# Attention, then a feed-forward network: the row of maxima transposed by VectorE, the ninth key tile added by GpSimd

## The chip, the cores and the metric

The kernel runs on one core of a Trainium2 chip. The core has five engines that each work through a queue of their own in order: TensorE (PE; its weight loads are shown apart as PEld), VectorE (DVE), ScalarE (ACT), GpSimd (POOL) and SyncE (SP), which here only issues transfers. They meet through semaphores. The metric is device microseconds of one execution.

## What is computed

Two stages, all in float32. The first is attention with pooled queries, for 8 batches of 8 heads, with 1152 keys of 64 numbers; two neighbouring queries are averaged, so 576 queries are left:

```python
q_pool = q.reshape(B, H, S // factor, factor, D).mean(axis=3)
scores = scale * np.matmul(q_pool, k.transpose(0, 1, 3, 2))
scores = scores - np.max(scores, axis=-1, keepdims=True)
attn = np.exp(scores)
attn = attn / (np.sum(attn, axis=-1, keepdims=True) + 1e-09)
return np.matmul(attn, v).astype(np.float32)
```

The second stage takes the result as 4608 tokens of 512 numbers through `h = x @ w_in`, `g = h - tanh(h)` and `g @ w_out`, with 2048 hidden numbers. The inputs are scaled so that the scores are large, which is why the maximum of each row has to be taken away before the exponential.

## The kernel before

**Pairs and units.** Heads are worked in pairs: 32 pairs, the two heads of a pair on partitions 0 to 63 and 64 to 127. A pair is worked in two halves of 288 queries. A half is nine key tiles of 128 keys; each gets one step of scores (`scores`), two units of a clock that the code counts. So a half is 18 units and a pair 36. All work beside the scores is hung on units by `add(u, f)`, some of it ahead of the unit's scores (`first`, then `early`), the rest behind. The table `units`, `row`, `steps` and `spots` of the last loop gives the unit of each piece of work, counted from the first unit of the pair that it is for: with -62 the work is done 62 units earlier, beside another pair's scores. `InOrder` makes every engine keep the order in which the code was run.

**Scores.** The numbers are split in a high and a low part (`hi` on ScalarE, `lo` on VectorE, which is `kq` less `hi`), and a step of scores is four kinds of product, for two heads each: `hi` by `hi`, `hi` by `lo`, `lo` by `hi`, and last `ones_k` by `mb`, which adds the negative maximum of each query to its column. `mb` holds the row of maxima as two rows per head, its high and its low part. ScalarE then takes the exponential out of PSUM into `p_f`.

**Maxima.** They come from products of the high parts alone (`max_part`): five query tiles by three key chunks, 15 a pair, hung on units of the pair before. VectorE reduces each over its keys (`mx<-ps`). `max_rows` then makes the row: VectorE reduces to ten columns (`nm`), TensorE transposes them with the identity into a PSUM tile (`ps<-ident,nm`), ScalarE and VectorE split the transpose in two parts (`mt`), and SyncE writes them to `m_dram` and reads them back to `mb` in four transfers.

**PSUM.** Scores, maxima, the transposed row, the outputs and the weight conversion all take their tiles from one pool of four (`ps_a`, two banks each). Whoever wants a fifth waits for the one to come free that was chosen when the program was built.

**Output and sums.** At a half's last unit TensorE multiplies the nine `p_f` by `v` (`pv`). GpSimd adds `p_f` tiles three by three, and the last group is two (`z_part`). After the second half's `pv`, `z_sums` sums over the keys by products with ones: four rounds, over the three sums `z` and over the ninth `p_f` itself, for two halves and two heads each. GpSimd also adds the two queries of a pool (`query_sums`, `kq<-q_n`), except for the first pair, and does part of the weight conversion (`w`, `w_hl`) that is spread over the pairs for the second stage.

**SyncE.** All loads and stores go through its queue in the order of the code.

Of the kernel before, what the change touches and what calls it, by code (L numbers as in the profile page):

```python
# [8 lines left out]
F32 = mybir.dt.float32  # L9
F32R = mybir.dt.float32r  # L10
I32 = mybir.dt.int32
AF = mybir.ActivationFunctionType
ALU = mybir.AluOpType
AX = mybir.AxisListType
# [29 lines left out]
def kernel(  # L44
# [17 lines left out]
    nc = tc.nc  # L62
    P = 128
    B, NP, _, _, SQ = q.shape
# [10 lines left out]
    dram = ctx.enter_context(tc.tile_pool(name="scratch", bufs=1, space=DRAM))  # L75

    ident = const.tile([P, P], F32, name="ident")
# [5 lines left out]
    ones = const.tile([P, 32], F32, name="ones")  # L83
# [3 lines left out]
    x_dram = dram.tile([NP, P, NTOK], F32, name="x_dram")  # L87
    z_dram = dram.tile([B, NP, 2, SQ], F32, name="z_dram")
    r_dram = dram.tile([B, NP, 2, SQ], F32, name="r_dram")
    m_dram = dram.tile([2, 10, 2, P], F32, name="m_dram")  # L90
    wi_dram = dram.tile([NF, P, 2, NP, P], F32, name="wi_dram")
    wo_dram = dram.tile([NF, P, 2, DM], F32, name="wo_dram")

# [41 lines left out]
    t, n = chunks.pop()  # L135
# [4 lines left out]
    with ExitStack() as actx:  # L140

        sm = actx.enter_context(tc.tile_pool(name="sm", bufs=2))
        op = actx.enter_context(tc.tile_pool(name="op", bufs=1))
# [7 lines left out]
        pe, act, dve, pool, sp = (InOrder(tc, e) for e in (nc.tensor, nc.scalar, nc.vector, nc.gpsimd, nc.sync))  # L151

        HQ = SQ // 2
        CH = S // 3
# [5 lines left out]


        mb = [op.tile([P, SQ], F32R, name=f"mb{i}") for i in range(2)]
        ones_k = op.tile([P, P], F32R, name="ones_k")
        for x in (*mb, ones_k):
            nc.gpsimd.memset(x.bitcast(F32), 0.0)
        for h in range(2):
            nc.gpsimd.memset(ones_k[64 * h:64 * h + 2].bitcast(F32), 1.0)


        at, first, early = {}, {}, {}  # L170

        def banks(dtype=F32):
            return ps_a.tile([P, 2, 512], dtype, name="ps")
# [3 lines left out]
        def add(u, f, *args, at=at):  # L177
            at.setdefault(u, []).append(lambda: f(*args))
# [22 lines left out]
        def query_sums(pi, eng):  # L201

            w = pairs[pi]
            eng.tensor_tensor(w.kq[:, 0:SQ], w.q_n[:, 0], w.q_n[:, 1], op=ALU.add)
            w.mx = sm.tile([P, 5, 2, 3], F32, name="mx")
            w.hi = hl.tile([P, KQ], F32R, name="hi")
            w.lo = hl.tile([P, KQ], F32R, name="lo")

# [8 lines left out]
        def max_part(u, pi, t, c):  # L217


            w = pairs[pi]  # L220
            ps = banks()
            q0 = min(t * P, SQ - P)
            mv = slice(SQ + c * CH, SQ + (c + 1) * CH)
            for h in range(2):
                r = slice(64 * h, 64 * h + 64)
                pe.matmul(ps[:, h, 0:CH], w.hi[r, q0:q0 + P], w.hi[r, mv], start=True, stop=True)
            add(u + 1, lambda: dve.tensor_reduce(w.mx[:, t, :, c], ps[:, :, 0:CH], axis=AX.X, op=ALU.max), at=first)

        def max_rows(u, pi, steps):

            w = pairs[pi]
            nm = sm.tile([P, 10], F32, name="nm")
            dve.tensor_reduce(nm, w.mx.rearrange("p t h c -> p (t h) c"), axis=AX.X, op=ALU.max, negate=True)
            mt = sm.tile([10, 2, P], F32R, name="mt")
            md = m_dram[w.i]

            def turn():
                w.ps_t = banks()[0:10, 0, 0:P]
                pe.transpose(w.ps_t, nm, ident)

            def hi():
                act.activation(mt[:, 0], w.ps_t, AF.Copy)

            def lo():
                dve.tensor_tensor(mt[:, 1], w.ps_t, mt[:, 0].bitcast(F32), op=ALU.subtract)

            def there():
                sp.dma_start(md, mt.bitcast(F32))

            def back():  # L250
                by_head = md.rearrange("(t h) s n -> h s t n", h=2)
                for h in range(2):
                    rows = w.mb[64 * h:64 * h + 2].bitcast(F32)
                    sp.dma_start(rows[:, 0:4 * P].rearrange("s (t n) -> s t n", n=P), by_head[h, :, 0:4])
                    sp.dma_start(rows[:, 4 * P:], by_head[h, :, 4, 5 * P - SQ:])
            add(u + 1, turn, at=first)
            add(u + 2, hi, at=first)
            add(u + 3, lo, at=first)
            add(u + steps[0], there)
            add(u + steps[1], back)  # L260

        def scores(w, half, kt, p):

# [21 lines left out]
        def pv(u, hf):  # L285

            w, ps = hf.w, banks()
            hf.o = ps[:, 0]
            for kt in range(KT):
                for h in range(2):  # L290
                    pe.matmul(hf.o[64 * h:64 * h + 64, 0:HQ], w.v[:, h, kt], hf.p[kt][:, h], start=(kt == 0),
                              stop=(kt == KT - 1), tile_position=(0, 64 * h))
            add(u + 1, o_out, w, hf, at=first)
            w.halves.append(hf)
            if hf.n == 1:
                z_sums(u, w, ps[:, 1])

        def z_sums(u, w, ps):

            parts = [[*hf.zs[:2], hf.p[-1], hf.zs[2]] for hf in w.halves]  # L300
            for g in range(4):
                for n in range(2):
                    for h in range(2):
                        r = 64 * h + 32 * n
                        pe.matmul(ps[r:r + 32, 0:HQ], ones, parts[n][g][:, h], start=(g == 0), stop=(g == 3), tile_position=(0, r))
            add(u + 1, z_out, u + 1, w, ps, at=first)

        def o_out(w, hf):
# [93 lines left out]
        for i, blk in enumerate(blocks):  # L402
            u = U * (i - 2) + 5 if i else 23
# [17 lines left out]
        for i, t in enumerate((wi, wi, wi, wo, wi, wo)):  # L421
            f = len(t)
# [3 lines left out]

        for pi in range(n_pair):
            u = pi * U
            units = dict(load=-80, query_sums=-62, hi=-55, lo=-36, load_v=-30)
            row, steps = -19, (5, 11)  # L430

            spots = [x for half, us in ((-54, (2, 4, 8, 10, 12, 14, 16)), (-36, (2, 4, 8, 10, 14, 16)))
                     for x in [(early, half)] + [(at, half + i) for i in us]]
            if pi == 0:
                units.update(load=-70, query_sums=-62, hi=-60, lo=-41, load_v=-40)
                spots = [(at, -60 + i) for i in range(15)]
                row, steps = -43, (3, 4)
            if pi == 1:
                units.update(load=-104)
            add(u + units["load"], load, pi)  # L440
            add(u + units["query_sums"], query_sums, pi, dve if pi < 1 else pool)
            for c in range(0, KQ, SQ):
                add(u + units["hi"], hi_part, pi, c, c + SQ)
            add(u + units["lo"], lo_part, pi)
            for i, (when, x) in enumerate(spots):
                add(u + x, max_part, u + x, pi, i // 3, i % 3, at=when)
            add(u + units["load_v"], load_v, pi)
            add(u + row, max_rows, u + row, pi, steps)

        def run(u, at=at):  # L450

            while at.get(u):
                at[u].pop(0)()

        for u in range(min(at), 0):
            run(u, first)
            run(u, early)
            run(u)
        z_groups = {kts[-1]: kts for kts in ((0, 1, 2), (3, 4, 5), (6, 7))}
        for u in range(end + 60):  # L460
            run(u, first)
            run(u, early)
            n, r = divmod(u, G)
            if u < end and r % 2 == 0:
                if r == 0:
                    hf = Half()
# [18 lines left out]
    pe, pool, sp = (InOrder(tc, e) for e in (nc.tensor, nc.gpsimd, nc.sync))  # L485
# [81 lines left out]
    for ci, (t0, n) in enumerate(chunks):  # L567
        x_h, x_l, _ = xs
        po = []
        for fc in range(NF):  # L570
# [3 lines left out]
            load = []  # L574
            if ci + 1 < len(chunks):
# [3 lines left out]
                load = [xs[2][(fc - x) // 3][i] for i, x in ((3, 3), (0, 0), (1, 2), (2, 2)) if (fc - x) % 3 == 0 and 0 <= fc - x < 3 * NP]  # L579
            for f in load:  # L580
                f()
            g = hidden(x_h, x_l, n, fc)
# [44 lines left out]
```

## Time and profile before

| | us |
|---|---|
| runs | 1634.25 to 1634.59, median 1634.48 |
| the profiled execution | 1634.2 |
| its span, first to last instruction | 1632.4 |
| TensorE busy | 1611.2 (99%) |
| VectorE, ScalarE, GpSimd busy | 1226.8, 1023.4, 873.3 |

TensorE's granted clock is full (1.000) over the span. The attention stage reaches to about 835 us, the feed-forward network takes the rest. In the timeline a row gives start and length in us, the engine, the line, the operation, the tiles written and read, and how many neighbouring instructions of one kind are merged in it; idle time before it stands in brackets, with what ended it. `L37` is the line of `InOrder`, so groups are told apart by their tiles. On TensorE the records of neighbouring matmuls overlap, so the time that one costs is read from start to start.

### The profile page before, as it was taken

What the parts mean: (1) busy time and instruction counts of PE and PEld (TensorE: products, weight loads), DVE (VectorE), ACT (ScalarE), POOL (GpSimd) and SP (SyncE); (2) the same over time, 40 slices, a digit from 0 to 9 for tenths busy, and PEclk for the clock granted to TensorE, in tenths of its full rate; (3) what the DMA queues carried; (4) which work ended last, traced back from release to release, by engine and by line L of the source; (5) the groups of instructions that cost most, each with busy time, mean ns of one, the idle gap of its engine ahead of it and who ended that gap; (6) DMA issues with size and microseconds to landing.
All of it is one profiled execution on the core that took longest, in us unless ns stands there. A gap on an engine that the chain in (4) does not pass through costs nothing.

```text
span 1632.4 us, 32106 instructions
## 1 busy us (share of the span) xinstructions
PE 1611.2 (99%) x12576; PEld 1246.3 (76%) x12576; DVE 1226.8 (75%) x1725; ACT 1023.4 (63%) x1865; POOL 873.3 (53%) x694
## 2 busy tenths in 40 slices
PE   6999999999999999999999999999999999999999
PEld 3777777777777777777778888888888888888898
DVE  7877778787777777777648776777777777777786
ACT  2656665666556656665566666666665766666786
POOL 2776767667667676676754243434343342423332
PEclk9999999999999999999999999999999999999999
DMA  3343443443434434344546111101010111000000
GB/s 142 121 139 117 140 134 108 127 130 133 127 108 142 134 114 126 123 140 146 157 177 229 39 39 35 31 26 53 26 53 26 39 40 39 27 33 20 33 21 27
DMA packets 72664, 147.86 MB, mean 91 GB/s; under 512 B 11136, under 2 KB 36672, under 8 KB 72512
## 3 DMA queue, kind: packets, MB, share of 16 engines
q1 hardware_dynamic: 72512, 145.80, 27.3%
q8 instruction: 99, 1.62, 0.4%
q14 instruction: 53, 0.43, 0.1%
HBM read 109.49 MB, written 36.27 MB: 89 GB/s over the span
## 4 chain that ended last, share of the span: by engine, by line
PE 97%; DVE 2%; ACT 0%; DMA 0%; issue 0%; ACTq 0%
PE ps L37 49%; PE ps_h L37 24%; PE ps_o L37 24%; DVE mx L37 1%; DMA q_n<-in_q_dram 0%; ACT hi L37 0%; ACT p_f L37 0%; DVE lo L37 0%; DVE kq L37 0%; DVE w L37 0%; DVE ps L37 0%; ACT x L562 0%; ACT z_s L37 0%; ACT mt L37 0%; DVE nm L37 0%
## 5 line engine op out<-in xcount | busy, mean ns | idle before, releaser
L37 DVE TENSOR_REDUCE mx<-ps 128x2 f32<-128x768 f32 x480 | 434.8, 951 | 139.0 <-PE ps L37 138.9
L37 POOL TENSOR_TENSOR g_lo<-g_s,g_hi 128x512 fp32r<-128x512 f32 (+1 forms) x160 | 190.7, 1192 | 483.1 <-ACT g_hi L530 445.0
L37 ACT ACTIVATE p_f<-ps 128x576 f32<-128x576 f32 x576 | 362.7, 650 | 83.5 <-PE ps L37 67.4
L37 POOL TENSOR_TENSOR z<-p_f 128x576 f32<-128x576 f32 x192 | 275.2, 1433 | 236.7 <-ACT p_f L37 236.7
L37 PE MATMUL ps<-hi 64*128 64x288 f32 (+1 forms) x2112 | 318.0, 355 | 13.4 <-ACT hi L37 8.3
L37 PE MATMUL ps_h<-x,wi 128*128 128x512 f32 (+1 forms) x1440 | 318.3, 370 | 0.0
L37 PE MATMUL ps_o<-wo,g_hi 128*128 128x512 f32 x1008 | 311.7, 391 | 0.0
L37 PE MATMUL ps<-p_f,v 128*64 128x288 f32 x2304 | 293.5, 409 | 0.1
L37 PEld LDWEIGHTS ps_h<-x,wi 128*128 128x128 f32 x1440 | 253.3, 188 | 50.3
L37 PEld LDWEIGHTS ps<-hi 64*128 64x128 f32 x2112 | 195.8, 188 | 79.8 <-DVE mx L37 22.9
L37 PEld LDWEIGHTS ps<-p_f,v 128*64 128x64 f32 x2304 | 159.8, 137 | 113.7 <-ACT p_f L37 12.2
L519 ACT ACTIVATE g_u<-ps_h 128x512 f32<-128x512 f32 (+1 forms) x160 | 88.8, 555 | 236.3 <-PE ps_h L37 236.3
L524 DVE SCALAR_TENSOR_TENSOR ps_w<-g_u,ps_h 128x512 f32<-128x512 f32 (+1 forms) x160 | 103.2, 645 | 157.6 <-ACT g_t L520 157.0
L37 PEld LDWEIGHTS ps_o<-wo,g_hi 128*128 128x128 f32 x1008 | 187.7, 188 | 39.0
L37 PE MATMUL ps_o<-wo,g_lo 128*128 128x512 f32 x504 | 196.4, 390 | 0.0
L37 POOL TENSOR_TENSOR z<-z,p_f 128x576 f32<-128x576 f32 x128 | 183.1, 1431 | 10.0
L37 ACT ACTIVATE o_s<-ps 128x288 f32<-128x288 f32 x64 | 26.3, 411 | 231.8 <-PE ps L37 231.8
L37 PE MATMUL ps<-lo,hi 64*128 64x288 f32 x1152 | 171.2, 294 | 0.0
L37 PE MATMUL ps<-hi,lo 64*128 64x288 f32 x1152 | 171.1, 293 | 0.0
L37 PE MATMUL ps<-mb,ones_k 64*128 64x288 f32 x1152 | 170.6, 292 | 0.0
L529 DVE COPY_PREDICATED g_s<-g_m,g_t 128x512 f32<-128x512 int32 (+1 forms) x160 | 115.1, 719 | 16.7 <-DVE g_s L528 0.5
L527 DVE SCALAR_TENSOR_TENSOR ps_w<-g_s,ps_w 128x512 f32<-128x512 f32 (+1 forms) x160 | 102.9, 643 | 16.6 <-ACT g_m L523 0.5
(70 smaller groups left out, 2248.3 us busy)
## 6 DMA issues: line engine op xcount, KB each, us to landing
q_n<-in_q_dram SPq DMA_DIRECT2D x32, 576.0 KB
kq<-in_k_dram SPq DMA_DIRECT2D x32, 576.0 KB
v<-in_v_dram SPq DMA_DIRECT2D x32, 576.0 KB
x_dram<-o_s SPq DMA_DIRECT2D x32, 288.0 KB
out_dram<-o_s SPq DMA_DIRECT2D x34, 256.0 KB
w_raw<-in_moe_w_in_dram SPq DMA_DIRECT2D x16, 512.0 KB
wi_dram<-w_hl SPq DMA_DIRECT2D x16, 512.0 KB
w_raw<-in_moe_w_out_dram SPq DMA_DIRECT2D x16, 512.0 KB
```

Of the source, the lines that this page charges most:

```text
L37: ins = self.tc.keep_in_program_order(f(*args, **kwargs))
L519: nc.scalar.activation(u, h, AF.Square)
L524: nc.vector.scalar_tensor_tensor(w, u, -P0, h, op0=ALU.add, op1=ALU.mult)
L527: nc.vector.scalar_tensor_tensor(w, s2, P2, w, op0=ALU.add, op1=ALU.mult)
L529: last = nc.vector.copy_predicated(s1, m.bitcast(I32), th).ins
```

## The change

`max_rows` no longer uses TensorE, ScalarE or `m_dram`. VectorE writes the ten columns into a zeroed tile of 32 columns, `nm`, and transposes it in blocks of 32 by 32 into `tr`. Column c of `nm` then lies in rows c, 32 + c, 64 + c and 96 + c of `tr`, and SyncE copies it from there to `mb`: ten transfers, one for each head and query tile, of four (or two) pieces of 32 numbers. The row is no longer split: `nm` is written in the rounded type that TensorE reads, `mb` holds one row per head, and `ones_k` has one row of ones per head. The transfers are hung 3 units after the reduction (1 for the first pair).

`z_part`'s last group becomes three tiles, and `z_sums` has three rounds. The loads of `q` and `k` move from unit -80 to -86, and the query sums from -62 to -71 (the second pair keeps -104 and -62, the first its own).

```diff
-        def max_rows(u, pi, steps):
+        def max_rows(u, pi, step):
             w = pairs[pi]
-            nm = sm.tile([P, 10], F32, name="nm")
-            dve.tensor_reduce(nm, w.mx.rearrange("p t h c -> p (t h) c"), axis=AX.X, op=ALU.max, negate=True)
-            mt = sm.tile([10, 2, P], F32R, name="mt")
...
-                pe.transpose(w.ps_t, nm, ident)
...
+            nm, tr = nms[w.i], sm.tile([P, 32], F32, name="tr")
+            dve.tensor_reduce(nm[:, 0:10], w.mx.rearrange("p h t c -> p (h t) c"), axis=AX.X, op=ALU.max, negate=True)
+            dve.transpose(tr, nm.bitcast(F32))
 
             def back():
+                for t in range(5):
+                    for h in range(2):
+                        row, c = w.mb[64 * h:64 * h + 1].bitcast(F32), 5 * h + t
+                        if t < 4:
+                            sp.dma_start(row[:, t * P:(t + 1) * P].rearrange("p (g n) -> p g n", n=32), tr[c:P:32])
+                        else:
+                            sp.dma_start(row[:, t * P:].rearrange("p (g n) -> p g n", n=32), tr[P - (SQ - t * P) + c:P:32])
+            add(u + step, back)
...
-            parts = [[*hf.zs[:2], hf.p[-1], hf.zs[2]] for hf in w.halves]
-            for g in range(4):
+            for g in range(3):
...
-            units = dict(load=-80, query_sums=-62, hi=-55, lo=-36, load_v=-30)
-            row, steps = -19, (5, 11)
+            units = dict(load=-86, query_sums=-71, hi=-55, lo=-36, load_v=-30)
+            row, step = -19, 3
...
-        z_groups = {kts[-1]: kts for kts in ((0, 1, 2), (3, 4, 5), (6, 7))}
+        z_groups = {kts[-1]: kts for kts in ((0, 1, 2), (3, 4, 5), (6, 7, 8))}
```

How this moves instructions is seen at three places. The first is TensorE between the two halves of a pair, the end of the first half's `pv` (64 rows, 288 queries) and the second half's first maxima (384 keys) and scores. Before:

```order
L37 MATMUL ps_4228<-p_f_4190,v_3761 64x288 x2
L37 MATMUL ps_4228<-p_f_4207,v_3761 64x288 [waits Activation_49]
L37 MATMUL ps_4228<-p_f_4207,v_3761 64x288
L37 MATMUL ps_4251<-ident_60,nm_4222 10x128 [waits DVE_49,PE_49]
L37 MATMUL ps_4255<-hi_4173 128x384 [waits PE_49,Activation_49]
L37 MATMUL ps_4255<-hi_4173 128x384
```

And now, for another pair:

```order
L37 MATMUL ps_1195<-p_f_1154,v_719 64x288 x2
L37 MATMUL ps_1195<-p_f_1169,v_719 64x288 [waits Activation_49]
L37 MATMUL ps_1195<-p_f_1169,v_719 64x288
L37 MATMUL ps_1220<-hi_1055 128x384 [waits PE_49,Activation_49]
L37 MATMUL ps_1220<-hi_1055 128x384
```

The transpose with the identity is gone, and with it the PSUM tile `ps_4251`.

The second place is a little later in the same half: its second step of scores, its second tile of maxima and the beginning of its third step. Before:

```order
L37 MATMUL ps_4274<-hi_3414 128x288 [waits Activation_49]
L37 MATMUL ps_4274<-hi_3414 128x288
L37 MATMUL ps_4274<-lo_3415,hi_3414 128x288 x2
L37 MATMUL ps_4274<-hi_3414,lo_3415 128x288 x2
L37 MATMUL ps_4274<-mb0_116,ones_k_118 128x288 x2
L37 MATMUL ps_4284<-hi_4173 128x384 [waits DVE_49]
L37 MATMUL ps_4284<-hi_4173 128x384
L37 MATMUL ps_4289<-hi_3414 128x288 [waits Activation_49]
```

And now:

```order
L37 MATMUL ps_4265<-hi_3327 128x288 [waits DVE_49]
L37 MATMUL ps_4265<-hi_3327 128x288
L37 MATMUL ps_4265<-lo_3328,hi_3327 128x288 x2
L37 MATMUL ps_4265<-hi_3327,lo_3328 128x288 x2
L37 MATMUL ps_4265<-mb0_115,ones_k_119 128x288 x2
L37 MATMUL ps_4275<-hi_4086 128x384 [waits Activation_49]
L37 MATMUL ps_4275<-hi_4086 128x384
L37 MATMUL ps_4290<-hi_3327 128x288 [waits DVE_49]
```

The order of the matmuls is the same, but the tiles come from others: the second tile of maxima waited for VectorE and the third step for ScalarE; now it is the other way round.

The third place is GpSimd's queue in a second half and up to the next half's first adds. Before:

```order
L37 TENSOR_TENSOR z_1648<-p_f_1602,p_f_1617 128x576
L37 TENSOR_TENSOR z_1648<-z_1648,p_f_1632 128x576
L37 TENSOR_TENSOR z_1700<-p_f_1651,p_f_1662 128x576
L37 TENSOR_TENSOR z_1700<-z_1700,p_f_1677 128x576
L37 TENSOR_TENSOR z_1733<-p_f_1703,p_f_1718 128x576
L37 TENSOR_TENSOR w_hl_1750<-w_1_1410,w_hl_1750 128x512
L37 TENSOR_TENSOR z_1847<-p_f_1799,p_f_1813 128x576
```

And now, again for another pair:

```order
L37 TENSOR_TENSOR z_1281<-z_1281,p_f_1262 128x576
L37 TENSOR_TENSOR z_1326<-p_f_1284,p_f_1295 128x576
L37 TENSOR_TENSOR z_1326<-z_1326,p_f_1311 128x576
L37 TENSOR_TENSOR z_1376<-p_f_1329,p_f_1344 128x576
L37 TENSOR_TENSOR z_1376<-z_1376,p_f_1359 128x576
L37 TENSOR_TENSOR kq_1277<-q_n_1276 128x576
L37 TENSOR_TENSOR w_hl_1374<-w_1_1029,w_hl_1374 128x512
L37 TENSOR_TENSOR z_1474<-p_f_1422,p_f_1440 128x576
```

The last `z` has a second add, and the query sum `kq`, which stood between the first and the second group of a first half, now stands between the halves.

More of the change, by code (lines that the diff above doesn't have):

```diff
@@ L89 @@
     r_dram = dram.tile([B, NP, 2, SQ], F32, name="r_dram")
-    m_dram = dram.tile([2, 10, 2, P], F32, name="m_dram")
     wi_dram = dram.tile([NF, P, 2, NP, P], F32, name="wi_dram")
@@ L162 @@
         mb = [op.tile([P, SQ], F32R, name=f"mb{i}") for i in range(2)]
+        nms = [op.tile([P, 32], F32R, name=f"nm{i}") for i in range(2)]
         ones_k = op.tile([P, P], F32R, name="ones_k")
-        for x in (*mb, ones_k):
+        for x in (*nms, *mb, ones_k):
             nc.gpsimd.memset(x.bitcast(F32), 0.0)
         for h in range(2):
-            nc.gpsimd.memset(ones_k[64 * h:64 * h + 2].bitcast(F32), 1.0)
+            nc.gpsimd.memset(ones_k[64 * h:64 * h + 1].bitcast(F32), 1.0)
         at, first, early = {}, {}, {}
@@ L204, in query_sums @@
             eng.tensor_tensor(w.kq[:, 0:SQ], w.q_n[:, 0], w.q_n[:, 1], op=ALU.add)
-            w.mx = sm.tile([P, 5, 2, 3], F32, name="mx")
+            w.mx = sm.tile([P, 2, 5, 3], F32, name="mx")
             w.hi = hl.tile([P, KQ], F32R, name="hi")
@@ L226, in max_part @@
                 pe.matmul(ps[:, h, 0:CH], w.hi[r, q0:q0 + P], w.hi[r, mv], start=True, stop=True)
-            add(u + 1, lambda: dve.tensor_reduce(w.mx[:, t, :, c], ps[:, :, 0:CH], axis=AX.X, op=ALU.max), at=first)
-        def max_rows(u, pi, steps):
+            add(u + 1, lambda: dve.tensor_reduce(w.mx[:, :, t, c], ps[:, :, 0:CH], axis=AX.X, op=ALU.max), at=first)
+        def max_rows(u, pi, step):
             w = pairs[pi]
-            nm = sm.tile([P, 10], F32, name="nm")
-            dve.tensor_reduce(nm, w.mx.rearrange("p t h c -> p (t h) c"), axis=AX.X, op=ALU.max, negate=True)
-            mt = sm.tile([10, 2, P], F32R, name="mt")
-            md = m_dram[w.i]
-            def turn():
-                w.ps_t = banks()[0:10, 0, 0:P]
-                pe.transpose(w.ps_t, nm, ident)
[L241 to L248, printed above, removed]
-            def back():
[L251 to L260, printed above, removed]
@@ L304, in z_sums @@
                         r = 64 * h + 32 * n
-                        pe.matmul(ps[r:r + 32, 0:HQ], ones, parts[n][g][:, h], start=(g == 0), stop=(g == 3), tile_position=(0, r))
+                        pe.matmul(ps[r:r + 32, 0:HQ], ones, w.halves[n].zs[g][:, h], start=(g == 0), stop=(g == 2),
+                                  tile_position=(0, r))
             add(u + 1, z_out, u + 1, w, ps, at=first)
@@ L436 @@
                 spots = [(at, -60 + i) for i in range(15)]
-                row, steps = -43, (3, 4)
+                row, step = -43, 1
             if pi == 1:
-                units.update(load=-104)
+                units.update(load=-104, query_sums=-62)
             add(u + units["load"], load, pi)
@@ L447 @@
             add(u + units["load_v"], load_v, pi)
-            add(u + row, max_rows, u + row, pi, steps)
+            add(u + row, max_rows, u + row, pi, step)
         def run(u, at=at):
```

## The prediction

> **What bounds the kernel now.** I read the page first: the busy shares, then the chain of work that ended last.
>
> ```profile
> PE 1611.2 (99%) x12576; PEld 1246.3 (76%) x12576; DVE 1226.8 (75%) x1725; ACT 1023.4 (63%) x1865; POOL 873.3 (53%) x694
> ...
> PE 97%; DVE 2%; ACT 0%; DMA 0%; issue 0%; ACTq 0%
> ```
>
> TensorE is busy 99% of the span and is 97% of the chain, so a microsecond taken off TensorE's queue is a microsecond off the time, as long as nobody else becomes late. "Busy" hides short waits, though, because a late matmul's record is only a longer one. So I measure slots, from the start of one instruction to the start of the next. The view of busy time by stretches shows one regular pair (columns: stretch, length, then busy time and count of PE, PEld, DVE, ACT, POOL; granted clock; DMA share; GB/s).
>
> ```profile
> 387.34:412.53 25.19, 25.19 (x283) 18.18 (x280) 19.24 (x23) 15.35 (x27) 17.86 (x13) 1.00 0.39 126
> ```
>
> A pair takes 25.19 us, and GpSimd works 17.9 us of it. The diff leaves the second half of the program (the FFN) as it is, so the question is what a pair will take. TensorE's timeline of that pair (start, length, what):
>
> ```profile
> 386.26 0.67 PE L37 MATMUL ps<-p_f,ones 128*32 128x288 f32 x8
> 386.74 0.67 PE L37 MATMUL ps<-z,ones 128*32 128x288 f32 x8
> 387.34 0.58 PE L37 MATMUL ps<-hi 64*128 64x384 f32 x4
> ...
> 389.48 0.56 PE L37 MATMUL ps<-hi 64*128 64x384 f32 x4
> 389.87 0.30 PE L37 MATMUL ps<-lo,hi 64*128 64x288 f32 x2
> 390.00 0.29 PE L37 MATMUL ps<-hi,lo 64*128 64x288 f32 x2
> ...
> 393.94 4.59 PE L37 MATMUL ps<-p_f,v 128*64 128x288 f32 x36
> 398.46 0.28 PE L37 MATMUL ps<-ident,nm 128*10 128x128 f32 x1
> 398.67 0.57 PE L37 MATMUL ps<-hi 64*128 64x384 f32 x4
> ...
> 399.88 0.29 PE L37 MATMUL ps<-mb,ones_k 64*128 64x288 f32 x2
> 400.17 0.70 PE L37 MATMUL ps<-hi 64*128 64x384 f32 x4
> 400.71 0.29 PE L37 MATMUL ps<-lo,hi 64*128 64x288 f32 x2
> ...
> 405.94 4.59 PE L37 MATMUL ps<-p_f,v 128*64 128x288 f32 x36
> 410.45 1.18 PE L37 MATMUL ps<-z,ones 128*32 128x288 f32 x16
> 411.45 0.67 PE L37 MATMUL ps<-p_f,ones 128*32 128x288 f32 x8
> ```
>
> **The change part by part.** The sum is made against the profiled execution's own 1634.2 us (span 1632.4 and 1.8 around it); the median of the runs, 1634.48, is 0.3 above it.
>
> *Fourth round of row sums.* The round over the ninth tile, `p_f,ones`, goes from 386.26 to 386.74: 0.48 us. Every one of the 32 pairs has one: 32 x 0.48 = 15.4 us less.
>
> *Transpose on TensorE.* It occupies 398.46 to 398.67, 0.21 us. Of 32, the first lies in the start-up, where TensorE waits anyway: 31 x 0.21 = 6.5 us less.
>
> *The tile it held.* The first half's scores and maxima go from 387.34 to 393.94: 6.60 us, with seven tiles of maxima. The second half, with eight, goes from 398.67 to 405.94: 7.27 us. A tile of maxima costs 389.87 - 389.48 = 0.39, less the 0.13 that two score matmuls take (389.87 to 390.00): 0.26. So 6.86 would do, and 0.41 is waiting. Two waits are visible: the maxima at 400.17 could have started at 400.01 (399.88 + 0.13), 0.16; and the next step takes 0.54 (400.17 to 400.71) instead of 0.39 or 0.40, about 0.14. Their cause stands on VectorE and ScalarE:
>
> ```profile
> 399.15 0.96 DVE L37 TENSOR_REDUCE mx<-ps 128x2 f32<-128x768 f32 x1 [2.43 <-PE ps L37]
> 400.60 0.28 DVE L37 TENSOR_TENSOR mt<-ps,mt 10x128 fp32r<-10x128 f32 x1 [0.48 <-ACT mt L37]
> ...
> 400.32 0.25 ACT L37 ACTIVATE mt<-ps 10x128 fp32r<-10x128 f32 x1
> ```
>
> The transposed row keeps one of the four PSUM tiles until VectorE's `mt` ends at 400.88. So the maxima at 400.17 take the tile of the half's first maximum, which VectorE gives up at 400.11, and VectorE itself stands idle 0.48 us for ScalarE's `mt`. With the row gone, the order shows these maxima waiting only for the output copy of the half before. I count 0.35 of the 0.41 (bounds: 0, and 0.41), since eight reductions of 0.9 us remain VectorE's own load of about 7.3 us. Pairs 0 to 29 have such a half: 30 x 0.35 = 10.5 us less.
>
> *Transpose on VectorE.* No row of before has this operation. The nearest is the reduction that feeds it:
>
> ```profile
> L37 DVE TENSOR_REDUCE nm<-mx 128x10 f32<-128x30 f32 x32 | 5.9, 184 | 1.1
> ...
> 20.65 0.18 DVE L37 TENSOR_REDUCE nm<-mx 128x10 f32<-128x30 f32 x1
> 20.75 1.95 DVE L37 TENSOR_TENSOR lo<-kq,hi 128x1728 fp32r<-128x1728 f32 x1
> 23.59 7.01 DVE L37 TENSOR_REDUCE mx<-ps 128x2 f32<-128x768 f32 x8 [0.70 <-PE ps L37]
> ```
>
> I take 0.2 us, between 0.1 and a GpSimd add's wait of 1.4. In a pair it stands where VectorE afterwards idles 2.43 us before 399.15, so it costs nothing on the path unless it passes 2.4. In the start-up `lo` can end near 22.9, and the eight reductions can follow at once instead of at 23.59, because ScalarE's `hi` no longer stands behind `mt`: 0.7 us less.
>
> *Ten transfers for five.* SyncE's queue issued four `mb` transfers in 1.17 us:
>
> ```profile
> 402.28 1.17 SPq L37 DMA_DIRECT2D mb<-m_dram  x4
> ...
> 22.92 0.36 SPq L37 DMA_DIRECT2D m_dram<-mt  x1
> 24.32 1.15 SPq L37 DMA_DIRECT2D mb<-m_dram  x4
> ```
>
> Ten are 2.9 us. They become ready with the transpose, about 395.6 in this pair, and so are out by about 398.5. The old way's write had landed 1.40 us after its issue (22.92 to 24.32), so the row is there by about 400 and is read after 412.5. Behind them wait the next loads, `q_n` and `kq`; they would be issued near 398.6, and GpSimd's query sum wants the first of them only after its sixth add, some 10 us later; the write of 1.40 us above is the nearest row for how long a transfer takes, and theirs are larger. Nothing there is near the path. TensorE's waits on transfers become ten a pair instead of four; 0 to 0.1 us a pair, I take 0.03: 1 us more.
>
> *Ninth tile on GpSimd.* One more add a half, on the engine that the last round of sums waits for. The second half's queue, with VectorE's `lo`:
>
> ```profile
> 401.18 1.42 POOL L37 TENSOR_TENSOR z<-p_f 128x576 f32<-128x576 f32 x1 [1.74 <-ACT p_f L37]
> 402.68 1.42 POOL L37 TENSOR_TENSOR z<-z,p_f 128x576 f32<-128x576 f32 x1
> ...
> 406.93 1.41 POOL L37 TENSOR_TENSOR z<-p_f 128x576 f32<-128x576 f32 x1
> 408.30 1.28 POOL L37 TENSOR_TENSOR w_hl<-w,w_hl 128x512 fp32r<-128x512 f32 x1
> ...
> 409.73 1.95 DVE L37 TENSOR_TENSOR lo<-kq,hi 128x1728 fp32r<-128x1728 f32 x1
> ```
>
> The first add starts 2.51 us after the half (401.18 - 398.67); the fifth ends at 408.34, the sixth would start at 408.43 (1.50 after 406.93, as 402.68 after 401.18) and end at 409.8, which is 11.15 after the half's start, or 11.0 without `mt` before the second exponential. TensorE wants it for the third round: 6.86 + 4.51 (405.94 to 410.45) + 1.00 (410.45 to 411.45) = 12.4. Margin 1.4 us, so nothing is lost in a regular pair. The query sum, moved to just after that add, and `w_hl` take 2.7 us more, to 13.7; the next half's first add can start at 12.95 + 2.3 = 15.3. That holds even if `lo` keeps both back for 1.95 (15.6). Room in total: 17.9 + 2 x 1.43 = 20.7 us of a pair of 24.1.
>
> The last two pairs are different. VectorE works on the FFN's first input there, and GpSimd's adds get longer:
>
> ```profile
> 804.08 1.42 POOL L37 TENSOR_TENSOR z<-p_f 128x576 f32<-128x576 f32 x1 [2.93 <-ACT p_f L37]
> 804.47 1.59 DVE L37 TENSOR_TENSOR q_n<-q_n 128x512 f32<-128x512 f32 x1 [0.68 <-DMA q_n<-r_dram]
> 805.58 1.75 POOL L37 TENSOR_TENSOR z<-z,p_f 128x576 f32<-128x576 f32 x1
> ...
> 810.93 1.86 POOL L37 TENSOR_TENSOR z<-p_f 128x576 f32<-128x576 f32 x1
> ...
> 811.29 1.18 PE L37 MATMUL ps<-z,ones 128*32 128x288 f32 x16
> ```
>
> Another add of 1.75 ends near 814.3, and the third round would want it at 811.29 - 0.21 + 0.99 = 812.1: a stall of 2.2 us. The last pair, without maxima, waits about 0.4: 2.6 us more (bounds 0 and 4).
>
> **Sum:** 15.4 + 6.5 + 10.5 + 0.7 - 1.0 - 2.6 = 29.5 us; 1634.2 - 29.5 = **1604.7 us**. Its own range: with the upper bounds 15.4 + 6.5 + 12.3 + 0.7 = 34.9, 1599.3; with 0.2 us of waiting recovered in each second half and the dearer bounds 15.4 + 6.5 + 6.0 + 0.7 - 4 - 3 = 21.6, 1612.6. With none recovered it is the first rival.
>
> **The rivals.** *VectorE paces the second half.* Eight reductions of 0.91 are 7.3 us, just the 7.27 that the half takes; then the tile was not the cause. For it: five of them stand without a gap. Against it: VectorE's idle 0.48 at the half's start. Then only rounds and transposes count: 15.4 + 6.5 + 0.7 - 3.6 = 19.0, 1615.
>
> *`lo` gets in ahead of the last adds.* In the start-up a GpSimd add that began 0.28 us after `lo` took 2.93 instead of 1.42:
>
> ```profile
> 32.57 1.95 DVE L37 TENSOR_TENSOR lo<-kq,hi 128x1728 fp32r<-128x1728 f32 x1
> 32.85 2.93 POOL L37 TENSOR_TENSOR z<-p_f 128x576 f32<-128x576 f32 x1 [23.79 <-ACT p_f L37]
> ```
>
> Before, `lo` ran after GpSimd's last add; now the sixth add is in its way. If `lo` begins before that add, the add ends 1.95 later, 0.55 past its margin: 30 x 0.55 = 16.5 back, 1621. Against it: `lo` comes 11.06 after the half's start now (409.73), and would come about 10.6; the sixth add starts at 9.6. The Trainium skill, "SBUF — State Buffer", section "SBUF: two separate sides", says that a VectorE instruction with two SBUF inputs and a GpSimd instruction share a port pair as an exclusive lock: whoever starts first keeps it for the whole instruction. The two rows agree with it, and so do 804.08 and 804.47, in the other order. By that rule `lo` waits here for the sixth add, which is the case in the sum.
>
> *GpSimd sets the pace; slower than before.* If besides `lo`'s 1.95 the six adds take 1.75 to 1.86 as near 810 (6 x 0.35 = 2.1), the last add is 4.05 - 1.4 = 2.65 late in every pair, against 1.06 won there: 30 x 2.65 = 79.5 off 29.5, 1684. It decides from a delay of 2.4 us on. Against it: regular pairs give VectorE only `lo` of this kind.
>
> **How the numbers follow.** The forecast (1599 to 1612) 0.65; VectorE's pace 0.14; `lo` first 0.11; more won than the sum allows 0.04; slower 0.05; nothing moved (a late load on GpSimd's queue eats it) 0.01. A measurement tells 0.2%, 3.3 us, from no change; the first four are all faster by more than that. For faster 0.91, same 0.03, slower 0.06. The range takes in VectorE's pace and most of `lo` first: 1598 to 1620.
>
> **What would show it.** Right: a round of sums gone and the last product of `z,ones` followed at once; second halves of 6.9 us from first matmul to `p_f,v`; a pair of about 24.15; GpSimd's sixth add ending over 1 us before the third round except at the end. Wrong: "PEld waits for POOL z" in regular pairs, or second halves still at 7.2.

## The result, and the profile after

The changed kernel takes 1611.39 us (median; 1610.90 to 1611.75) against 1634.52 for the kernel before on the same chip (1634.25 to 1634.59; the 1634.48 given further up is the median of the first three of these four runs). The ratio is 0.9857, its 95% interval 0.9843 to 0.9872: 23.1 us less. The forecast was 1604.7, so 6.7 us of the expected gain are missing. The time lies inside the range of 1598 to 1620.

The page of the changed kernel, busy time first and then the chain of work that ended last:

```profile
PE 1584.2 (98%) x12288; PEld 1233.6 (77%) x12288; DVE 1235.9 (77%) x1725; ACT 1015.9 (63%) x1833; POOL 1016.9 (63%) x760
...
PE 49%; ACT 0%; issue 0%
```

TensorE has 288 matmuls fewer: 256 of the fourth rounds and 32 transposes. GpSimd has gained 144 us of work. The chain is traced over only half the span here, all of it on TensorE, so it doesn't say where the rest went. I cut both spans instead into the pieces that the prediction used, from the start of a piece's first matmul to the start of the next piece's:

| piece of TensorE's time, us | before | after | difference | forecast |
|---|---|---|---|---|
| start-up, to the first `p_f,v` | 41.12 | 44.49 | +3.37 | -0.7 |
| scores and maxima, 30 second halves | 218.04 | 210.79 | -7.25 | -10.5 |
| the same, 31 first halves | 203.46 | 204.04 | +0.58 | +1.0 (waits on transfers, all halves) |
| transposes | 6.35 | 0 | -6.35 | -6.5 |
| sums with ones, pairs 0 to 29 | 62.32 | 47.77 | -14.55 | -14.4 |
| the same, last two pairs | 5.15 | 6.59 | +1.44 | +1.6 |
| all the rest | 1095.98 | 1095.89 | -0.09 | 0 |
| span | 1632.42 | 1609.57 | -22.85 | -29.5 |

Four of the six terms came within 0.5 us. Two did not: the start-up (4.1 us off) and the second halves (3.2 us off). Together they are 7.3 us, and the other four give 0.7 of it back: that is the missing gain.

**A regular pair** took 25.19 us and now takes 24.24 (view by stretches, columns as in the prediction):

```profile
387.46:411.70 24.24, 24.24 (x274) 17.75 (x272) 19.33 (x24) 15.10 (x26) 22.44 (x16) 1.00 0.41 130
```

GpSimd is busy for 22.44 of it. The forecast said 20.7; the rest is explained below. TensorE's timeline of the second half:

```profile
389.18 0.58 PE L37 MATMUL ps<-hi 64*128 64x384 f32 x4
...
393.42 0.67 PE L37 MATMUL ps<-hi 64*128 64x384 f32 x4
393.93 0.29 PE L37 MATMUL ps<-lo,hi 64*128 64x288 f32 x2
...
396.20 4.59 PE L37 MATMUL ps<-p_f,v 128*64 128x288 f32 x36
400.72 1.66 PE L37 MATMUL ps<-z,ones 128*32 128x288 f32 x24
402.31 0.57 PE L37 MATMUL ps<-hi 64*128 64x384 f32 x4
```

The half goes from 389.18 to 396.20: 7.02 us, where 7.27 stood before and 6.9 was forecast. The three rounds are one row of 24 products without a gap, 1.59 us. Some steps still wait: 393.42 to 393.93 is 0.51, where the prediction counted 0.39 for a tile of maxima with its first score matmuls.

GpSimd and VectorE in the same stretch:

```profile
397.31 1.42 POOL L37 TENSOR_TENSOR z<-p_f 128x576 f32<-128x576 f32 x1
398.81 1.41 POOL L37 TENSOR_TENSOR z<-z,p_f 128x576 f32<-128x576 f32 x1
400.01 2.03 DVE L37 TENSOR_TENSOR lo<-kq,hi 128x1728 fp32r<-128x1728 f32 x1
400.18 3.13 POOL L37 TENSOR_TENSOR kq<-q_n 128x576 f32<-128x576 f32 x1
...
404.62 1.44 POOL L37 TENSOR_TENSOR z<-p_f 128x576 f32<-128x576 f32 x1
```

The sixth add ends at 400.22, 11.04 us after the half's start (forecast: 11.0 to 11.15). The third round would want it at 400.72 + 2 x 1.593 / 3 = 401.8, so about 1.6 us are left (forecast: 1.4; two runs below find 1.4 too). `lo` starts about when the sixth add ends (the records overlap by 0.2), and then holds back the query sum, which takes 3.13 instead of 1.43. The next half's first add starts 15.44 after the half's start; the prediction had 15.3, or 15.6 if `lo` held the query sum. By groups over the whole program (columns: busy us, mean ns of one, idle before):

```profile
L37 POOL TENSOR_TENSOR kq<-q_n 128x576 f32<-128x576 f32 x31 | 88.5, 2856 | 29.6 <-DVE ps L37 25.0 <-DMA q_n<-in_q_dram 4.6
L37 DVE STREAM_TRANSPOSE tr<-nm 128x32 f32<-128x32 f32 x32 | 6.8, 212 | 5.5 <-DMA wi_dram<-w_hl 1.9 <-DVE nm L37 0.9 <-DMA v<-in_v_dram 0.9
```

Before, the query sum's mean was 1429 ns. The blocked time is counted as busy, which is the 1.7 us that GpSimd's 22.44 exceeds the forecast by. VectorE's transpose takes 0.21 us, against the 0.2 that the prediction took.

The prediction had named "PEld waits for POOL z" as a sign that it was wrong. It is there, in the view of waits and in this very pair (columns of the first: us in total, times, longest):

```profile
PEld ps L37 <- POOL z L37: 13.6, 28, 1.8
...
PE ps L37 <- POOL z L37: 1.3, 1, 1.3
```

```profile
400.72 1.13 PEld L37 LDWEIGHTS ps<-z,ones 128*32 128x32 f32 x24 [0.44 <-POOL z L37]
```

But it is no stall: TensorE's row above has no gap at 400.72. The 0.44 us are time in which only the loading of weights stands still, while TensorE is still at `p_f,v`. What tells is the second row: TensorE itself waited for `z` once, 1.3 us, in the last but one pair. The sign was badly chosen.

**The start-up.** The prediction quoted SyncE's queue of before up to the four `mb` transfers at 24.32. This is what came behind them, and what hung on it (timeline of before):

```profile
25.51 0.36 SPq L37 DMA_DIRECT2D w_raw<-in_moe_w_in_dram  x1
...
29.62 0.63 ACT L37 ACTIVATE ps<-w_raw 128x512 f32<-128x512 f32 x1 [6.24 <-DMA w_raw<-in_moe_w_in_dram]
...
31.96 0.69 DVE L37 SCALAR_TENSOR_TENSOR w<-ps,w 128x512 int32<-128x512 int32 x1
...
32.71 0.93 PE L37 MATMUL ps<-hi 64*128 64x384 f32 x4 [0.63 <-DVE w L37]
```

And the same places of the changed kernel:

```profile
21.28 5.49 SPq L37 DMA_DIRECT2D mb<-tr  x10
22.95 7.00 DVE L37 TENSOR_REDUCE mx<-ps 128x2 f32<-128x768 f32 x8
...
26.81 0.40 SPq L37 DMA_DIRECT2D v<-in_v_dram  x1
27.25 0.43 SPq L37 DMA_DIRECT2D w_raw<-in_moe_w_in_dram  x1
...
32.62 0.62 ACT L37 ACTIVATE ps<-w_raw 128x512 f32<-128x512 f32 x1 [21.69 <-DMA w_raw<-in_moe_w_in_dram]
...
33.28 0.70 DVE L37 TENSOR_SCALAR ps<-ps 128x512 f32<-128x512 f32 x1 [3.33 <-ACT ps L37]
...
34.73 0.69 DVE L37 SCALAR_TENSOR_TENSOR w<-ps,w 128x512 int32<-128x512 int32 x1
...
35.48 0.93 PE L37 MATMUL ps<-hi 64*128 64x384 f32 x4 [4.05 <-DVE w L37]
```

VectorE's eight reductions do start 0.64 us sooner (22.95, before 23.59), as forecast. But the ten transfers occupy SyncE's queue for 5.49 us, not 2.9. The first pair's `v`, which before was asked for at 2.61 us, now stands behind them and reads ahead of `w_raw`, which is asked for 1.74 us later (27.25 against 25.51) and lands 3.0 later: ScalarE's conversion of it into a PSUM tile starts at 32.62 instead of 29.62. Three operations of VectorE work on that tile, and `w<-ps,w` is the last of them. Before, they followed VectorE's reductions at once, and `w` ended at 32.65 (31.96 + 0.69). Now VectorE waits 3.33 us for ScalarE's conversion, and `w` ends at 35.42 (34.73 + 0.69). It is what TensorE's next tile of maxima waits for in both rows, 0.63 us before and 4.05 now. So TensorE waits for a weight block that belongs to the second stage, and restarts 2.77 us late. (The first exponentials stand behind the same conversion in ScalarE's queue, but they end at 34.35, ahead of `w`.) In a regular pair the ten take as long and hurt nobody (SyncE's queue):

```profile
386.50 5.33 SPq L37 DMA_DIRECT2D mb<-tr  x10
391.87 0.40 SPq L37 DMA_DIRECT2D q_n<-in_q_dram  x1
```

**The last two pairs.** TensorE and GpSimd in the last but one:

```profile
787.04 1.65 PE L37 MATMUL ps<-z,ones 128*32 128x288 f32 x20
788.51 1.40 POOL L37 TENSOR_TENSOR z<-z,p_f 128x576 f32<-128x576 f32 x1
...
789.97 0.68 PE L37 MATMUL ps<-z,ones 128*32 128x288 f32 x4 [1.28 <-POOL z L37]
```

The sums wait for the sixth add, 3.54 us instead of 1.59: a stall of 1.95 (forecast 2.2).

### The profile page after: what moved, and what is told of

Same layout as the page of the kernel before. It is cut to its first block, busy times and chain, and to the rows that moved or that the text cites. A ratio compares the mean times of both kernels' runs of the same rounds, so it can differ in the third digit from the quotient of the medians.

```text
span 1609.6 us, 31923 instructions
## 1 busy us (share of the span) xinstructions
PE 1584.2 (98%) x12288; PEld 1233.6 (77%) x12288; DVE 1235.9 (77%) x1725; ACT 1015.9 (63%) x1833; POOL 1016.9 (63%) x760
## 3 DMA queue, kind: packets, MB, share of 16 engines
q8 instruction: 97, 1.59, 0.4%
## 5 line engine op out<-in xcount | busy, mean ns | idle before, releaser
L37 ACT ACTIVATE p_f<-ps 128x576 f32<-128x576 f32 x576 | 356.6, 651 | 78.9 <-PE ps L37 56.4
L37 POOL TENSOR_TENSOR z<-z,p_f 128x576 f32<-128x576 f32 x192 | 273.3, 1423 | 15.0
```

The lines of the kernel that those rows point to most:

```text
L37: ins = self.tc.keep_in_program_order(f(*args, **kwargs))
```

## The experiments

My theory after the result had three parts. The start-up loss is the order in SyncE's queue. The second half's gain comes from the PSUM tile that the row held. GpSimd has a margin of about one add, no more, and pays for it only at the end. The rivals are two of the prediction (VectorE's reductions pace the second half; `lo` gets in ahead of the last adds) and one more: the edits on loads and query sums are what counts.

**The two parts apart.** First the row alone, on the sums and units of before.

```diff
-            units = dict(load=-86, query_sums=-71, hi=-55, lo=-36, load_v=-30)
+            units = dict(load=-80, query_sums=-62, hi=-55, lo=-36, load_v=-30)
...
-            for g in range(3):
+            for g in range(4):
...
-        z_groups = {kts[-1]: kts for kts in ((0, 1, 2), (3, 4, 5), (6, 7, 8))}
+        z_groups = {kts[-1]: kts for kts in ((0, 1, 2), (3, 4, 5), (6, 7))}
```

> Of the change the row of maxima alone (VectorE's transpose, one part, ten transfers); four rounds of sums, two tiles in the last add and the old times of loads and query sums. Theory (the parts add up): transposes -6.4, second halves -7.3, start-up +3.4, the rest nothing: 1634.5 - 10.3 = 1624.2; second halves 7.02 us. Rival (the second halves became shorter for another reason, the query sums' or the adds' new place): second halves stay near 7.27, 1631.5.

Measured: 1623.72 us, ratio 0.9932 (0.9917 to 0.9946). In its trace the start-up is 3.31 us longer than before, the second halves 6.47 shorter (one of them takes 7.86 us, the others about 7.02), the first halves 0.36 shorter, and the transposes' 6.35 are gone: 10.0 in all. Next the sums alone (the same lines the other way round, on the row of before).

> Of the change the sums alone: ninth tile added by GpSimd, three rounds, loads and query sums sooner; the row of maxima as before. Theory (the parts add up): rounds 30 x 0.485 = -14.6, the last two pairs +1.4, second halves stay at 7.27: 1634.5 - 13.1 = 1621.4. Rival (the second halves became shorter through this part): second halves near 7.02, 1614.

Measured: 1622.89 us, ratio 0.9934 (0.9917 to 0.9951); of eight executions seven took 1621.63 to 1624.24, one 1634.06, and the profiled one 1621.75. Sums of pairs 0 to 29: 14.55 less; of the last two: 1.86 more; second halves +0.28, start-up -0.21; the span 12.48 less. The two spans' gains, 10.01 and 12.48, add up to 22.49 of the 22.85. By the medians it is 11.28 and 12.11, against 23.13. So in the sum the parts are independent, the start-up loss belongs to the row, and so does the second half's gain.

**The start-up.** In the changed kernel I let SyncE fetch the first pair's `v` ahead of the ten transfers:

```diff
-                units.update(load=-70, query_sums=-62, hi=-60, lo=-41, load_v=-40)
+                units.update(load=-70, query_sums=-62, hi=-60, lo=-41, load_v=-44)
```

> The change, with one load moved: the first pair's values are fetched ahead of the ten transfers of its row of maxima, as before the change. Theory (SyncE's queue): the start-up lost 3.4 us because the values and the first raw weights wait in the queue behind the ten transfers; without the values ahead of them the weights, issued near 26.8, land 4.1 us later as before (25.51 to 29.62), near 30.9 instead of 32.6; first product of p_f and v near 42.8 instead of 44.5, time 1609.7. Rival (the ten transfers themselves come too late for the scores, or the transpose does): no gain, 1611.4.

Measured: 1609.67 us (0.9846; 0.9829 to 0.9862), the start-up 42.75. Then the first weight block too:

```diff
-            add(u, w_block, u, *blk)
+            add(-44 if i == 1 else u, w_block, u, *blk)
```

> The change, with the first pair's values and also the first raw weights fetched ahead of the ten transfers. Theory (SyncE's queue): the weights are there long before ScalarE wants them, the start-up gains the 0.7 us that the prediction had counted instead of losing 3.4; first product of p_f and v near 40.4, time 1607.3. Rival: no gain over the change, 1611.4.

Measured: 1608.48 us (0.9839; 0.9824 to 0.9853), the start-up 40.82, below the 41.12 of before. Its timeline:

```profile
21.27 5.48 SPq L37 DMA_DIRECT2D mb<-tr  x10
...
27.38 0.62 ACT L37 ACTIVATE ps<-w_raw 128x512 f32<-128x512 f32 x1 [16.47 <-DVE mx L37]
...
31.31 0.69 DVE L37 SCALAR_TENSOR_TENSOR w<-ps,w 128x512 int32<-128x512 int32 x1
...
32.05 0.93 PE L37 MATMUL ps<-hi 64*128 64x384 f32 x4 [0.63 <-DVE w L37]
```

The ten transfers are as long as ever. `w_raw` is converted at 27.38, before VectorE has finished its reductions, and VectorE's three operations follow them at once again: `w` ends at 32.00. TensorE restarts at 32.05, 0.66 sooner than before, which is what VectorE's earlier reductions give. With `v` alone moved it restarts at 33.87, so the restart follows the place of `w_raw` in the queue, and the cause of the loss is shown. Of the 0.66 only 0.30 are left at the first `p_f,v`, and nothing in the two runs further down with the same loads (41.23 and 41.09). The total is 1.2 above the expected 1607.3: 0.4 of it in the start-up, 0.36 in the last two pairs' sums, 0.4 between the profiled execution (1608.07) and the median.

**The row's copy out of PSUM.** The kernel before, with its transposes and its row in two parts, but the row copied out of PSUM one and two units sooner:

```diff
-            add(u + 2, hi, at=first)
-            add(u + 3, lo, at=first)
+            add(u + 1, hi, at=first)
+            add(u + 1, lo, at=first)
```

> The kernel before, with one thing moved: ScalarE and VectorE copy the transposed row out of PSUM at the beginning of the second half, ahead of the first exponential and of the first maximum, instead of behind them. TensorE's transpose stays. Theory (the held tile): the second halves fall from 7.27 to about 7.02 although the transpose, its copies and all eight reductions are still there: 30 x 0.25 = 7.3 us, 1635.0 - 7.3 = 1627.7. Rival (VectorE's eight reductions, or the transpose itself, set the second half's length): second halves stay at 7.27, 1635.0.

Measured: 1626.98 us against 1634.67, ratio 0.9951 (0.9934 to 0.9967). Second halves fall from 7.27 to 7.01 us, 7.59 in all, with everything else of before in place:

```profile
396.12 0.28 DVE L37 TENSOR_TENSOR mt<-ps,mt 10x128 fp32r<-10x128 f32 x1 [2.35 <-ACT mt L37]
396.33 0.93 DVE L37 TENSOR_REDUCE mx<-ps 128x2 f32<-128x768 f32 x1
```

`mt` ends at 396.40 and frees its tile before VectorE has the half's first reduction; before, it stood behind that reduction. So the row's late copy was the cause, and 0.25 a half is all that it cost; the same eight reductions now go with halves of 7.01, so they alone did not set the 7.27. The run doesn't tell two things apart that both went: the tile comes free sooner, and VectorE no longer stands idle for ScalarE's `mt` (0.48 us in the pair of the prediction) between two reductions. It also shows that a third of the change's gain was to be had by moving two lines of the old kernel.

**What is left in the second halves.** Of the 0.41 us that the prediction called waiting, 0.24 went. VectorE has five reductions in a row in this half (its groups in one half of the changed kernel):

```profile
389.67 0.96 DVE L37 TENSOR_REDUCE mx<-ps 128x2 f32<-128x768 f32 x1 [1.83 <-PE ps L37]
390.91 1.82 DVE L37 TENSOR_REDUCE mx<-ps 128x2 f32<-128x768 f32 x2 [0.28 <-PE ps L37]
393.09 4.42 DVE L37 TENSOR_REDUCE mx<-ps 128x2 f32<-128x768 f32 x5 [0.36 <-PE ps L37]
```

```diff
-            spots = [x for half, us in ((-54, (2, 4, 8, 10, 12, 14, 16)), (-36, (2, 4, 8, 10, 14, 16)))
+            spots = [x for half, us in ((-54, (2, 4, 6, 10, 12, 14, 16)), (-36, (2, 4, 8, 10, 14, 16)))
```

> The changed kernel, but the second half's tiles of maxima hang on units 0, 2, 4, 6, 10, 12, 14 and 16 instead of 0, 2, 4, 8, 10, 12, 14 and 16, so that VectorE has four reductions, a step of scores without maxima, and four reductions, instead of three and five. Theory (what is left of waiting in the second halves, 7.02 us against the 6.86 that the forecast worked out, comes from VectorE's five reductions of 0.88 in a row, where TensorE offers one each 0.79): 0.05 to 0.15 us less in each of 30 halves, 1.5 to 4.5 us in all, about 1608.4. Rival (the 7.02 are TensorE's own time, or another engine's): second halves stay at 7.02 and the time at 1611.4.

Behind the first one its groups are three and four now:

```profile
389.76 2.69 DVE L37 TENSOR_REDUCE mx<-ps 128x2 f32<-128x768 f32 x3 [0.28 <-PE ps L37]
392.69 3.55 DVE L37 TENSOR_REDUCE mx<-ps 128x2 f32<-128x768 f32 x4 [0.24 <-PE ps L37]
```

Measured: 1609.67 us (0.9848; 0.9832 to 0.9865). The second halves are 0.93 shorter in all, 0.03 each, the first halves 0.30; another 0.51 is in the start-up, which this edit doesn't touch and which moves by as much in the other runs of the last series. Neither expectation is met: the run of five is a small part of what is left. TensorE's slots, averaged over the 30 halves, say the same. A tile of maxima together with the delay of the scores behind it costs 0.26, 0.31, 0.19, 0.37, 0.19 and 0.36 us in the changed kernel (six tiles that have scores behind them), and 0.26, 0.31, 0.23, 0.30, 0.27 and 0.28 with the maxima spread. The see-saw goes, the mean stays: 0.28 and 0.275, not the 0.26 that the prediction read from one tile. From the start of its first reduction to the end of its last (389.67 to 397.51) VectorE is busy for 7.20 us and idle for only 0.64, so it may be the bound of this half by now. That was not tested by itself and stays open.

**GpSimd's margin.** One add more in each second half (its result is overwritten by the next):

```diff
             hf.zs.append(z)
+            if kts[0] == 3 and hf.n == 1:
+                for _ in range(1):
+                    pool.tensor_tensor(z, hf.p[0], hf.p[1], op=ALU.add)
             pool.tensor_tensor(z, hf.p[kts[0]], hf.p[kts[1]], op=ALU.add)
```

> The change, with one add more on GpSimd in every second half, between its first and second group (its result is overwritten, the output stays). Theory (margin, and the shared port in the order of starting): the sixth add would start at 400.2 of the profiled pair instead of 398.8, and lo, ready at 400.0, now comes ahead of it: the sixth add ends near 403.5 instead of 400.2, the third round wants it at 401.7, a stall of 1.8 us in each of 30 pairs and some 2 more in the last two: 1611.4 + 56 = 1667. Rival 1 (a plain margin, no port): the add ends at 401.6, no stall in a regular pair: 1611.4 + 3 = 1614. Rival 2 (GpSimd sets the pace already): 32 x 1.42 = 45, 1657.

Measured: 1667.25 us in two executions, ratio 1.0198 (1.0178 to 1.0219), slower than before.

```profile
394.07 4.59 PE L37 MATMUL ps<-p_f,v 128*64 128x288 f32 x36
...
396.68 1.41 POOL L37 TENSOR_TENSOR z<-p_f 128x576 f32<-128x576 f32 x1
397.88 2.02 DVE L37 TENSOR_TENSOR lo<-kq,hi 128x1728 fp32r<-128x1728 f32 x1
398.17 2.99 POOL L37 TENSOR_TENSOR z<-z,p_f 128x576 f32<-128x576 f32 x1
...
398.59 1.65 PE L37 MATMUL ps<-z,ones 128*32 128x288 f32 x20
...
401.22 0.68 PE L37 MATMUL ps<-z,ones 128*32 128x288 f32 x4 [0.98 <-POOL z L37]
```

The extra 1.42 alone would have used up the margin and no more. But with it the last add comes after `lo`, takes 2.99 instead of 1.41 and ends at 401.16. That is 7.09 us after the half's `p_f,v` began (394.07), where the changed kernel has 4.02 (400.22 - 396.20): 3.07 later. The sums take 3.23 us instead of 1.59, so 1.64 of it are paid and the margin was 1.43. Over 30 pairs it is 49.9 us. This is the outcome of the prediction's slower rival, but by another way: one add more and `lo` ahead of the last, where that rival had all six adds longer.

**`lo` first.** In the changed kernel `lo` is put one unit sooner, which takes it ahead of three weight operations in VectorE's queue:

```diff
-            units = dict(load=-86, query_sums=-71, hi=-55, lo=-36, load_v=-30)
+            units = dict(load=-86, query_sums=-71, hi=-55, lo=-37, load_v=-30)
```

> The change, with lo one unit sooner, so that VectorE does it ahead of the three operations of the weight conversion instead of behind them. This is the rival of the prediction in which lo comes before the sixth add. Theory (port lock, margin 1.5 us): lo is ready near 397.6 of the profiled pair, waits for the fifth add (to 398.7), holds the sixth until about 400.7, which then ends near 402.1, 0.4 after the third round wants it: 30 x 0.4 = 12, 1623. Rival (no lock, or more margin): 1611.4.

Measured: 1613.63 us in two executions (0.9870; 0.9850 to 0.9890).

```profile
396.06 4.59 PE L37 MATMUL ps<-p_f,v 128*64 128x288 f32 x36
...
397.28 3.12 DVE L37 TENSOR_TENSOR lo<-kq,hi 128x1728 fp32r<-128x1728 f32 x1
398.65 3.00 POOL L37 TENSOR_TENSOR z<-z,p_f 128x576 f32<-128x576 f32 x1
...
400.58 1.81 PE L37 MATMUL ps<-z,ones 128*32 128x288 f32 x24
```

`lo` finds the fifth add (397.17 to 398.58) running and waits for it (3.12 instead of 1.95), then the sixth add waits for `lo`. It ends at 401.65, 5.59 us after `p_f,v` began (396.06) instead of 4.02: 1.57 later. The sums wait 0.16 a pair, so the margin was again 1.41. That is 4.6 us over 30 pairs, where 12 were expected. The start-up is 2.4 shorter, which was not looked into. The rival's mechanism is real. Its price is less than a third of the 0.55 that the prediction gave it: the add ends 1.57 later, not `lo`'s whole 1.95. The edit moved `lo` by one unit; an earlier place was not tried.

**The loads and query sums sooner.** The changed kernel with the query sums back at the old unit:

```diff
-            units = dict(load=-86, query_sums=-71, hi=-55, lo=-36, load_v=-30)
+            units = dict(load=-86, query_sums=-62, hi=-55, lo=-36, load_v=-30)
...
-                units.update(load=-104, query_sums=-62)
+                units.update(load=-104)
```

> The change, with the query sums at their old place in the first half (unit -62, and the second pair's load and sums as before the change). Theory (margin): in the first half the last add ends 1.4 us later than without them but the first add starts sooner, since lo no longer holds back a query sum ahead of it; the second half's first add starts no later than 0.1 us, so nothing is lost: 1611.4, 1612.0 at most. Rival (the query sums had to move for the ninth tile to fit): 0.5 us and more in each pair, 1627.

Measured: 1611.52 us (1610.63 to 1612.45; ratio 0.9857, 0.9843 to 0.9872). Moving the query sums changes nothing that these runs can tell. The loads were not moved back by themselves.

**The end.** In the second halves of the last two pairs the last group is two tiles again, and TensorE takes their ninth tile:

```diff
+                if r == 0:
+                    hf.last = hf.n == 1 and n // 2 >= n_pair - 2
+                    if hf.last:
+                        z_groups = {2: (0, 1, 2), 5: (3, 4, 5), 7: (6, 7)}
+                    else:
+                        z_groups = {2: (0, 1, 2), 5: (3, 4, 5), 8: (6, 7, 8)}
...
+            parts = [[*hf.zs[:2], *hf.p[-1:] * hf.last, hf.zs[2]] for hf in w.halves]
```

> The changed kernel, but in the second halves of the last two pairs the last group of sums is two tiles again, and TensorE takes the ninth tile of these two halves itself in a shortened fourth round (four products instead of eight; it costs about 0.24 us a pair). In the changed kernel the sums of the last two pairs take 6.59 us, against 2 x 1.593 = 3.19 without a stall. Theory (GpSimd's sixth add is what is late there): the two take about 4.8 us, the time falls by 1.8 to 1609.6. Rival (GpSimd is late there anyway, because its other adds are longer beside VectorE): the stall stays, and the shortened round comes on top: 1611.4 to 1611.9.

Measured: 1609.15 us (0.9844; 0.9830 to 0.9859), 2.24 below the changed kernel. Of that, 0.49 is in the start-up, which this edit doesn't touch. The two pairs' sums take 5.04 us instead of 6.59. Nearly all of that is the last but one: 2.08 instead of 3.54. The last pair's piece is 2.96 instead of 3.05: its stall of about 0.5 us is gone, but four products and the next stage's wait for the row sums to be copied out (0.8 us) stand in it.

**Together.** First the two loads and the end, then the spread maxima as well.

> The changed kernel with the first pair's v and the first raw weight block fetched ahead of the ten transfers (1608.48 when run alone) and with the last two pairs' sums as in the run on the end of the attention stage. If both are independent terms: 1608.5 - 1.9 = 1606.6. If the stall at the end stays: 1608.5 to 1609.

Measured: 1606.40 us (1606.07 to 1606.43; ratio 0.9826, 0.9811 to 0.9841).

> As the run before, and the second half's maxima spread in two fours. If VectorE's five reductions in a row are what is left of waiting there: 3 us below that run, 1603.6. If not: the same 1606.6.

Measured: 1605.50 us (1605.42 to 1606.03; ratio 0.9822, 0.9807 to 0.9836). This beats both kernels: 29.3 us below the one before on that chip, and 5.9 below the changed one's median, which is from another chip. The spread is worth about 1 us, a third of what the theory asked.

## Why the prediction was right, and where it was not

- *Fourth round, 15.4.* Right: 14.55 in 30 pairs, 0.485 each.
- *Transposes, 6.5.* Right: 6.35.
- *The tile it held, 10.5.* The mechanism was right as far as the run with the row copied out sooner can show: the row held in PSUM was what cost time, by its tile, by VectorE's wait for `mt`, or by both. The size was not: 7.25, or 0.24 a half instead of 0.35. The step that failed is "A tile of maxima costs 389.87 - 389.48 = 0.39, less the 0.13 ... So 6.86 would do, and 0.41 is waiting". One tile stood for eight; the mean is 0.28, and what the eight reductions cost TensorE after the tile is free is not in the 0.26. "Eight reductions of 0.9 us remain" was said, and given 0.06 a half; it would have needed 0.16.
- *Start-up, 0.7.* The step that failed is "Ten transfers for five": "Ten are 2.9 us ... Nothing there is near the path". They are 5.3 to 5.5. And the sentence looked at a regular pair alone. In the start-up the first pair's `v` and `w_raw` stand behind them, and behind `w_raw` ScalarE's conversion, VectorE's `w` and TensorE's next tile of maxima. The prediction named what is queued behind the transfers as if the first pair were like the rest. It cost 3.4 us instead of bringing 0.7. VectorE's 0.64 was there, and with both loads ahead TensorE restarts 0.66 sooner; but the prediction took this for time saved, and at the first `p_f,v` the three runs with these loads are 0.30 and 0.03 sooner and 0.11 later than before.
- *Waits on transfers, 1.0.* Not seen: with the row alone, the first halves are 0.36 shorter. The 0.58 of the changed kernel are three halves of 7.05, 6.75 and 7.04 us among others of about 6.60 (before, two of 6.83 and 6.82); in the last of the three VectorE's `lo` had been held by GpSimd's query sum and its reductions came late.
- *Ninth tile, margin 1.4.* Right: 1.43 and 1.41 by the two runs that use it up, and one add more costs 1.64 us a pair.
- *Last two pairs, 2.6.* Right. The last but one waits 1.95 (2.2 forecast). The last one's piece is 3.05, before 2.98: it saves a round of 0.48 and waits 0.55 (0.4 forecast).
- *`lo` and the sixth add.* Right: `lo` waits for it. The Trainium skill's page "SBUF — State Buffer", section "SBUF: two separate sides", has whoever starts first keep the port pair for its whole instruction; the rows at 400.01 and 400.18 agree, and so do those of the run with one more add and of the run with `lo` first. Where an add ends while both engines have the next one ready, VectorE's went first in the rows of these three kernels.
- *The chances.* The four that end faster add up to 0.94, where 0.91 was given for faster; the prediction doesn't say why.

## What to carry to other kernels

A piece of work that is priced in a regular stage has to be priced again in the first one, queue by queue: name what stands behind it there and who waits for that, also on other engines. A wait is best sized over all its instances: 0.02 us a tile, because one tile was read instead of all, became 0.16 a half where 0.06 had been allowed, and that is the 3 us missing there. And an engine that is 63% busy can be one instruction away from setting the pace, when its last result is the one that is waited for.

## What the runs showed of the hardware

Ten transfers inside SBUF of at most four pieces of 128 bytes each held SyncE's queue for 0.53 to 0.55 us apiece (5.33 and 5.49 for ten), while the four from DRAM that they replace took 0.29 each (1.17 for four). What makes them dearer was not taken apart.

TensorE's matmuls in the start-up come at half the rate, with the granted clock shown as full. The same stretch of time, before and after (stretches, columns as above), with TensorE busy throughout:

```profile
38.50:42.00 3.50, 3.50 (x44) 2.90 (x42) 3.08 (x4) 2.79 (x5) 3.42 (x4) 1.00 0.00 0
```

```profile
38.50:42.00 3.50, 3.50 (x30) 3.50 (x32) 2.36 (x3) 1.47 (x3) 2.19 (x3) 1.00 0.02 5
```

A kind of product of scores takes 0.24 there and 0.13 later. In the kernel before the faster rate comes at about 38.8 us, in the changed one at about 43.1, after TensorE's gap of 4.05 us. The rest of the start-up's loss goes with it: from TensorE's restart to the first `p_f,v` it takes 9.01 us instead of 8.41, 0.6 on top of the 2.77. In the traces of the other runs this stretch takes 8.2 to 9.4 us (7.2 with `lo` first), so half a microsecond of start-up between two runs says little about their edits. The Trainium skill, "TensorE: Matmul & The Clock Gate", section "Part 1: The HAM clock gate", describes an array that is clocked at half rate until it has been busy for some 3.4 us, and again after as long an idle window. The ratio of 0.24 to 0.13 agrees; the granted clock in the profile, 1.00 in both rows, doesn't show it, and the slow stretch here, from TensorE's restart on and with short gaps in it, lasts 7.6 us.
